# Two issuing queues and a re-scored order for the first loads of an attention kernel with two MLPs

## The chip, the cores and the metric

The kernel runs on one core of a Trainium2 chip. The metric is device time in microseconds (us), the median of several runs; lower is better. PE is the matrix engine (TensorE), DVE is VectorE, ACT is ScalarE, POOL is GpSimd, SP is SyncE, whose only work here is to start DMA transfers. Each engine runs its own list of instructions strictly in order; semaphores make one engine wait for another or for a transfer.

## What is computed

A strided sparse attention (4 batches, 8 heads, 576 tokens, 64 wide) feeds two MLPs one after the other. Half of the heads see the last 32 tokens, the other half every 32nd token.

```python
scores = scale * np.matmul(q, k.transpose(0, 1, 3, 2))
mask_local = (rel >= 0) & (rel < stride)
mask_strided = (rel >= 0) & (pos[None, :] % stride == pos[:, None] % stride)
...
attn = np.exp(scores - max); attn = attn / (sum + 1e-09)
x = (attn @ v), heads side by side          # 2304 tokens x 512
h = x @ w_in;  g = s * relu(h)**2 + b;  x = g @ w_out          # 512 -> 2048 -> 512
h = x @ w_in2; g = where(h >= 1, h, where(h <= -1, 0, (h + 1)**2 / 4)); out = g @ w_out2
```

## The kernel before

All matrix products of the MLPs are done three times on pairs of a high and a low part (hi*hi, hi*lo, lo*hi), so that float32 accuracy comes out of a faster matmul format. Lines 843 to 845 are these three in the first MLP, 1088 to 1090 in the later stages. Weights arrive as 64-bit numbers in tiles named `raw` (512 KB each, three buffers, loaded at L439) and are decoded into a hi and a lo tile: ACT (L443, into `dt`), DVE (L445, L447), a copy to the hi tile (L424, on ACT or DVE), a subtraction to the lo tile (L459, on DVE or POOL). `w0...` tiles are w_in pieces, `w1...` tiles are w_out pieces.

The 2304 tokens are cut into six units of 384. Unit 0 can enter the first MLP only when five attention tiles are complete: three strided tiles of batch 0 (inputs `in_strd`) and two local ones (`in_loc`). I number them 0 to 4; tile 5 is the next local one, whose scores also use spare PSUM banks. An attention tile is a chain:

- scores on PE: a mask matmul (L721, L733) and many small ones (L726 strided, L741 local);
- softmax: row maximum (DVE L749), subtraction (DVE L752), exponential (ACT L755), row sum (DVE L756), reciprocal (DVE L757), product (L758, DVE or POOL);
- transpose on PE (L767), copy to `pt` (L424);
- times the values on PE (L783 strided, L793 local);
- split into `xh` (ACT, L424) and `xl` (DVE, L826).

The third strided tile takes its keys and queries from small tiles `k` and `q`, filled by three DMAs and by POOL copies out of tiles 0 and 1. The inputs of the first tiles borrow buffers meant for later data, so load targets carry names such as `xh`, `xl`, `w0hx`, `w1hx`: `xh` and `xl` receive keys and queries, `w0hx`, `w0lx`, `w1hx`, `w1lx` receive values. The function `load` (L568) issues all of them on SP.

Nothing of the order is written by hand. Every step is recorded by `Issue.op` with its possible engines and an estimated length; `order` walks the steps back from the end to give each a due time; `draw` then simulates the engines 96 times with random shifts of the due times, always taking the step that can start first (earlier due time on a tie), and the draw whose PE ends first is emitted by `emit`. The simulation also holds a model of PE's clock (`Pulse`), and where PE would wait in the first 45 us it puts up to `MOST` matmuls on a constant tile (`busy`, L715, `warm_t`), which keep PE active and compute nothing. Ten more of these open the program (L1320). In `emit`, SP's loads planned for the first 32 us (`CALM`) also wait for an earlier load, so that not too much is in flight. Apart from that, each transfer uses one of eight completion semaphores in turn (DMAHW0 to DMAHW7), and one that reuses a semaphore may first wait until the transfer that used it last has landed.

## Time and profile before

| | us |
|---|---|
| median of three runs | 827.94 (826.4 to 828.8) |
| the profiled execution, whole | 829.0 |
| its span in the trace | 827.2 |
| PE busy | 813.6 (98%) |
| DVE busy | 627.0 (76%) |
| ACT busy | 516.4 (62%) |
| POOL busy | 113.5 (14%) |

The profiled execution's own time is 1.8 us above its span; that part lies outside the trace. Busy PE time contains the fillers of L715 and L1320 and every matmul that ran at the lower clock, so it is not all useful work. In the chain of work that ended last, PE has 94%, DMA 3%, SP's issuing 1% and ACT 1%. Times below count from the start of the span.

### The profile page before, as it was taken

Reading aid. Unit: us, or ns where it says so; the run is one execution under the profiler, and the core shown is the slowest. Engines: PE = TensorE matmul, PEld = TensorE weight load, DVE = VectorE, ACT = ScalarE, POOL = GpSimd, SP = SyncE. Lnnn points to the kernel's source line nnn. Section 1 sums busy time; section 2 is a strip of 40 time slices with the busy share of each in tenths; the row PEclk is TensorE's granted clock in tenths of the full one; section 3 lists DMA queues with packets and bytes.
Section 4 is the critical chain, followed back from the end, with each engine's and each line's share of the span. In section 5 each row is a group of like instructions: output and inputs, shape, how many; then the busy total and the mean of one; then the engine's idle time right before and its main releaser. Section 6 shows DMA issues by size and latency. Waiting matters only on the chain.

```text
span 827.2 us, 17722 instructions
## 1 busy us (share of the span) xinstructions
PE 813.6 (98%) x6295; PEld 788.1 (95%) x6301; DVE 627.0 (76%) x1314; ACT 516.4 (62%) x1052; POOL 113.5 (14%) x233
## 2 busy tenths in 40 slices
PE   7998999999999999999999999999999999999998
PEld 3688999999999999999999999999999999999998
DVE  4888429888867468689889987997477987466966
ACT  2576445565656676558676677855486855667553
POOL 4041104343321013030221000000000000000000
PEclk8999999999999999999999999999999999999999
DMA  6895265899777467899989999888988789888882
GB/s 222 269 300 189 86 204 178 277 298 302 270 267 255 149 238 268 299 305 351 340 307 337 294 399 353 253 251 274 305 253 254 253 251 298 282 253 253 253 267 95
DMA packets 105524, 218.25 MB, mean 264 GB/s; under 512 B 14196, under 2 KB 27868, under 8 KB 105436
## 3 DMA queue, kind: packets, MB, share of 16 engines
q1 hardware_dynamic: 95196, 180.41, 67.4%
q0 software_dynamic: 10240, 36.71, 11.8%
q8 instruction: 51, 0.84, 0.4%
q14 instruction: 37, 0.30, 0.1%
HBM read 170.93 MB, written 46.14 MB: 262 GB/s over the span
## 4 chain that ended last, share of the span: by engine, by line
PE 94%; DMA 3%; SPq 1%; ACT 1%; POOL 0%; issue 0%; DVE 0%; ACTq 0%
PE acc L1088 8%; PE acc L1090 8%; PE acc L1089 8%; PE h L843 8%; PE h L845 8%; PE h L844 8%; PE side L1088 6%; PE side L1090 6%; PE side L1089 6%; PE acc L843 4%; PE acc L844 4%; PE acc L845 4%; PE h L1088 3%; PE h L1090 3%; PE h L1089 3%; PE side L793 1%
## 5 line engine op out<-in xcount | busy, mean ns | idle before, releaser
L843 PE MATMUL h<-xh,w0hx 128*128 128x384 f32 x192 | 65.9, 343 | 1.4 <-ACT w0hx L424 1.4
L845 PE MATMUL h<-xh,w0lx 128*128 128x384 f32 x192 | 65.0, 339 | 0.8 <-POOL w0lx L459 0.8
L843 PE MATMUL h<-xh,w0h 128*128 128x384 f32 x192 | 65.6, 342 | 0.0
L489 POOL DMA_DIRECT2D dw<-pp x60 | 43.5, 725 | 155.7 <-DVE pp L487 129.4
L844 PE MATMUL h<-xl,w0hx 128*128 128x384 f32 x192 | 64.7, 337 | 0.0
L845 PE MATMUL h<-xh,w0l 128*128 128x384 f32 x192 | 64.4, 335 | 0.0
L844 PE MATMUL h<-xl,w0h 128*128 128x384 f32 x192 | 64.3, 335 | 0.0
L871 ACT ACTIVATE t<-h 128x384 f32<-128x384 f32 x50 | 24.5, 490 | 45.7 <-PE h L845 45.5
L883 DVE TENSOR_TENSOR gl<-t,gh 128x384 fp32r<-128x384 f32 x36 | 20.0, 555 | 26.9 <-ACT gh L424 26.9
L843 PEld LDWEIGHTS h<-xh,w0hx 128*128 128x128 f32 x192 | 36.1, 188 | 2.2 <-ACT w0hx L424 1.7
L845 PEld LDWEIGHTS h<-xh,w0lx 128*128 128x128 f32 x192 | 36.2, 189 | 1.2 <-POOL w0lx L459 1.1
L843 PEld LDWEIGHTS h<-xh,w0h 128*128 128x128 f32 x192 | 36.1, 188 | 0.5
L844 PEld LDWEIGHTS h<-xl,w0hx 128*128 128x128 f32 x192 | 36.2, 189 | 0.0
L844 PEld LDWEIGHTS h<-xl,w0h 128*128 128x128 f32 x192 | 36.1, 188 | 0.0
L845 PEld LDWEIGHTS h<-xh,w0l 128*128 128x128 f32 x192 | 36.0, 188 | 0.0
L424 ACT ACTIVATE gh<-w1h 128x384 fp32r<-128x384 f32 x48 | 24.9, 523 | 16.2 <-PE acc L1090 6.8
L1135 DVE TENSOR_TENSOR gl<-w1h,gh 128x384 fp32r<-128x384 f32 x48 | 26.5, 555 | 11.1 <-ACT gh L424 10.9
L843 PE MATMUL acc<-gh,w1h 128*128 128x384 f32 (+1 forms) x96 | 33.5, 349 | 0.0
L843 PE MATMUL acc<-gh,w1hx 128*128 128x384 f32 (+1 forms) x96 | 32.9, 343 | 0.0
L845 PE MATMUL acc<-gh,w1l 128*128 128x384 f32 (+1 forms) x96 | 32.5, 339 | 0.3 <-POOL w1l L459 0.3
L844 PE MATMUL acc<-gl,w1hx 128*128 128x384 f32 (+1 forms) x96 | 32.6, 339 | 0.0
L845 PE MATMUL acc<-gh,w1lx 128*128 128x384 f32 (+1 forms) x96 | 32.5, 338 | 0.0
(608 smaller groups left out, 2812.2 us busy)
## 6 DMA issues: line engine op xcount, KB each, us to landing
dw<-pp POOLq DMA_DIRECT2D x60, 512.0 KB, 5.2
w0h<-dw SPq DMA_DIRECT2D x84, 256.0 KB
w0l<-dw SPq DMA_DIRECT2D x84, 256.0 KB
w0hx<-dw SPq DMA_DIRECT2D x84, 256.0 KB
w0lx<-dw SPq DMA_DIRECT2D x84, 256.0 KB
raw<-in_w_ins SPq DMA_DIRECT2D x32, 512.0 KB
raw<-in_w_outs SPq DMA_DIRECT2D x32, 512.0 KB
kb<-dw SPq DMA_DIRECT2D x56, 256.0 KB
```

The lines of the kernel that those rows point to most:

```text
L424: e.activation(out=out, in_=in_, func=AF.Copy)
L489: op(lambda e: e.dma_start(out=dw[o][i][qs].rearrange("q p w n -> p q (w n)"), in_=y.tile[:, 0:nq].bitcast(F32).rearrange("p q w n -> p q ...
L793: e.matmul(out=pv[blk].tile[half(par), hp, c:c + 32], lhsT=v4(pos)[half(blk), s, 2 * hp + par, :], rhs=pt.tile[half(blk), 2 * par + pos, r ...
L843: e.matmul(out=acc, lhsT=wh, rhs=ah, start=first, stop=False)
L844: e.matmul(out=acc, lhsT=wh, rhs=al, start=False, stop=False)
L845: e.matmul(out=acc, lhsT=wl, rhs=ah, start=False, stop=last)
L871: op(lambda e: e.activation(out=c(t), in_=c(p), func=AF.Relu), [act(n)], [p], [t])
L883: op(lambda e: e.tensor_tensor(out=c(gl), in0=c(t), in1=c(gh).bitcast(F32), op=SUB), [pool(n)] + [dve2(n)], [t, gh], [gl])
L1088: e.matmul(out=dst, lhsT=wh, rhs=ah, start=opens and first, stop=False, skip_group_check=not opens)
L1089: e.matmul(out=dst, lhsT=wh, rhs=al, start=False, stop=False, skip_group_check=not opens)
L1090: e.matmul(out=dst, lhsT=wl, rhs=ah, start=False, stop=last, skip_group_check=not opens)
L1135: op(lambda e, g=g, hi=hi, lo=lo: e.tensor_tensor(out=lo.tile[:, 0:n], in0=g.tile, in1=hi.tile[:, 0:n].bitcast(F32), op=SUB), [dve2(n)], [ ...
```

## The change

Four things change, all in the planner and in `load`:

1. Loads of at most 128 KB that belong to tiles 0 to 2 may be issued by ACT as well as SP; the planner picks the engine that is free first.
2. The loads of the first unit are no longer kept in the fixed sequence `EARLY`: each target tile has a line of its own (`own`), and due times decide. Later loads stay in one line.
3. Of the 96 draws the best 24 are kept, each is replayed with five positions of the clock model's window, and the lowest sum wins. In the replay SP may run further ahead (`AHEAD_SP`).
4. Constants of the model: `MOST` from 8 to 12, ACT's start from 1.4 to 1.2, `FETCH` from 4.5 to 4.0, a limit on open transfers (`LANES`), and a longer issue time for small transfers.

```diff
-DRAWS, JITTER = 96, 1.0
+DRAWS, JITTER, KEPT, PHASES, AHEAD_SP = 96, 1.0, 24, (0.0, 0.7, 1.4, 2.0, 2.7), 4.0
-FILL, MOST = 45.0, 8
+FILL, MOST = 45.0, 12
...
-BEGIN = {"sp": 0.7, "act": 1.4, "dve": 0.5, "pool": 6.4, "pe": 5.2}
+BEGIN = {"sp": 0.7, "act": 1.2, "dve": 0.5, "pool": 6.4, "pe": 5.2}
...
-BLOCK, FETCH, FETCH_AT, FETCH_LONG = 256, 4.5, 1.5, 1.3
-CALM, FLIGHT = 32.0, 2.5
+BLOCK, FETCH, FETCH_AT, FETCH_LONG = 256, 4.0, 1.5, 1.3
+CALM, FLIGHT, LANES = 32.0, 2.5, 8
...
-        return min((self.draw(seed) for seed in range(DRAWS)), key=lambda x: x[0])[1]
+        drawn = sorted((x for x in map(self.draw, range(DRAWS)) if x[1]), key=lambda x: x[0])[:KEPT]
+        return min((sum(self.replay(took, phase) for phase in PHASES), n, took) for n, (_, took) in enumerate(drawn))[2]
...
+    def earliest(self, o, e, more, t, deep):
+        free = self.free
+        at = max(free[e], o.ready, t)
+        if "port" in more:
+            at = max(at, free["port"])
+        elif more and e != "pool":
+            at = max(at, self.lanes[-LANES])
+        if e == "sp":
+            at = max(at, free["dma"] - deep)
...
+    def replay(self, took, phase):
+        self.begin(phase)
+        for o in sorted(self.ops, key=lambda o: (took[o][0], o.n)):
+            _, e, n = took[o]
+            _, d, lag, *more = next(x for x in o.engs if x[0] == e)
+            self.put(o, e, self.earliest(o, e, more, self.room(o), AHEAD_SP), d, lag, more, n)
+        return self.free["pe"]
...
     def load(i, y, parts, size, piece):
         first = bool(w_loads) and not held
-        o = op(lambda e: [e.dma_start(out=f(), in_=x) for f, x in parts], [dma(size, piece, len(parts))], part=[y],
-               line=a_line, after=[w_loads[k] for k in HOLD] if first else ())
+        issue = (0.45 if size > 128 * 1024 else 0.62) * len(parts)
+        queues = ("sp", "act") if i < 3 and size <= 128 * 1024 else ("sp",)
+        o = op(lambda e: [e.dma_start(out=f(), in_=x) for f, x in parts], [dma(size, piece, 0.0, issue, q) for q in queues], part=[y],
+               line=a_line if brought else own.setdefault(y, []), after=[w_loads[k] for k in HOLD] if first else ())
```

The order moves at three places that matter here. In the changed program line numbers are 23 higher from `load` on.

**The first loads.** On SP, before, the first loads of the program stand like this; `in_strd` and `in_loc` are the attention inputs, and the sizes are partitions x float32 words:

```order
L568 DMA xh5_1_189<-in_strd 128x764 x2
L568 DMA xl5_2_192<-in_strd 128x2x764
L568 DMA w0hx_3_194<-in_strd 64x2x256 x2
L568 DMA k3_4_219<-in_strd 64x2x72 x2
L568 DMA q3_5_222<-in_strd 128x2x72
L568 DMA w0lx_6_227<-in_strd 64x2x256 x2
L568 DMA w1hx_7_257<-in_strd 18x256 x2
L568 DMA w1hx_7_257<-in_strd 64x256
L568 DMA w1hx_7_257<-in_strd 54x1x256
L568 DMA xh4_8_271<-in_loc 128x896
L568 DMA xl4_9_280<-in_loc 128x896
```

In the changed program SP has this at the same place:

```order
L591 DMA xh5_1_189<-in_strd 128x764 x2
L591 DMA xl5_2_195<-in_strd 128x2x764
L591 DMA xh4_8_234<-in_loc 128x896
L591 DMA xl4_9_274<-in_loc 128x896
L591 DMA xh3_12_285<-in_loc 128x896
L591 DMA xl3_13_315<-in_loc 128x896
L591 DMA xl2_57_334<-in_loc 128x896
L591 DMA xh2_56_399<-in_loc 128x896
```

And ACT, ahead of its first exponential (L778, L755 before), now has these, with the semaphores that they wait for:

```order
L591 DMA k_4_192<-in_strd 64x2x72 x2
L591 DMA q_5_197<-in_strd 128x2x72
L591 DMA w0hx_199<-in_strd 64x2x256 x2
L591 DMA w0lx_202<-in_strd 64x2x256 [waits DMAHW1_49]
L591 DMA w0lx_202<-in_strd 64x2x256 [waits DMAHW3_49]
L591 DMA w1hx_227<-in_strd 18x256 [waits DMAHW4_49]
L591 DMA w1hx_227<-in_strd 18x256 [waits DMAHW5_49]
L591 DMA w1hx_227<-in_strd 64x256 [waits DMAHW7_49]
L591 DMA w1hx_227<-in_strd 54x1x256 [waits DMAHW0_49]
L778 ACTIVATE sm_207<-sm_207 128x4x128 [waits DVE_49]
```

All eleven small loads of tiles 0 to 2 moved to ACT, and the six big loads of tiles 3 to 5 follow the strided ones directly on SP. The semaphore DMAHW3 is that of the load of `xl5`, the last DMAHW0 that of `xh4`.

**PE around the second step of the first MLP.** `h_80` is that step's result, `h_64` and `sx_62` belong to tile 5, `warm_t` is the filler. Before, between the second step and the values of tile 5:

```order
L845 MATMUL h_80_781<-xh0_177,w0l_77_510 128x384
L715 LDWEIGHTS warm_t_73
L715 MATMUL h_64_816<-warm_t_73 128x512
...
L767 MATMUL h_64_816<-id_t_69,sx_62_702 128x128 x4
...
L715 MATMUL side_66_836<-warm_t_73 128x512
...
L793 MATMUL side_66_836<-pt_65_817,qx_58_748 64x32 x2
```

Now the second step is followed by the scores of a later strided tile and then by the third step:

```order
L868 MATMUL h_80_786<-xh0_177,w0l_77_565 128x384
L744 LDWEIGHTS idb_t_72
L744 MATMUL side_172_816<-bias_t_71,idb_t_72 128x256
...
L749 MATMUL side_172_816<-xh5_168_762 54x54
...
L866 MATMUL h_88_846<-xh0_177,w0h_84_680 128x384
L867 MATMUL h_88_846<-xl0_178,w0h_84_680 128x384
```

The fillers there are gone, and the transpose of tile 5 now stands ahead of the first step.

**ACT at the decoding of the seventh w_in piece.** `raw_138` is its load, `raw_146` is a w_out piece, `w0hx_136` the hi tile made from the first. Before:

```order
L443 ACTIVATE dt_139_1154<-raw_138_1052 128x512
L443 ACTIVATE dt_147_1172<-raw_146_1107 128x512
L755 ACTIVATE sx_193_1122<-sx_193_1122 128x4x128
L871 ACTIVATE t_129_1148<-h_128_1147 128x384
L875 ACTIVATE t_129_1148<-t_129_1148 128x384
L424 ACTIVATE w0hx_136_1053<-dt_139_1154 128x512
```

Now:

```order
L898 ACTIVATE t_129_1144<-t_129_1144 128x384
L445 ACTIVATE gh_130_1145<-t_129_1144 128x384
L445 ACTIVATE w0hx_136_1065<-dt_139_1172 128x512
L464 ACTIVATE dt_147_1225<-raw_146_1116 128x512
L778 ACTIVATE sx_193_1182<-sx_193_1182 128x4x128
```

The copy into `w0hx_136` moved from behind the instruction that waits for `raw_146` to ahead of it.

## Rows read from the trace of the kernel before

**Rows 1.** Windows: length, busy PE PEld DVE ACT POOL, clock, DMA share, GB/s.

```profile
0.00:36.57 36.57, 29.00 (x584) 17.45 (x589) 23.29 (x65) 14.43 (x36) 10.13 (x45) 0.91 0.75 246
36.57:75.00 38.43, 35.90 (x390) 31.63 (x386) 31.28 (x69) 27.08 (x60) 12.72 (x22) 0.96 0.87 253
75.00:823.50 748.50, 748.45 (x5330) 739.02 (x5328) 571.91 (x1180) 474.66 (x957) 90.64 (x166) 1.00 0.80 266
```

**Rows 2.** Waits of PE: total us, times, longest.

```profile
PE acc L741 <- DMA xh<-in_loc: 2.8, 1, 2.8
PE h L843 <- ACT w0hx L424: 1.4, 1, 1.4
PE acc L741 <- DMA xl<-in_loc: 1.1, 1, 1.1
PE h L845 <- POOL w0lx L459: 0.8, 1, 0.8
```

**Rows 3.** SP's issues in order of time: start, us, line, transfer, count.

```profile
1.65 0.43 SPq L568 DMA_DIRECT2D xl<-in_strd  x1
4.00 1.95 SPq L568 DMA_DIRECT2D w0hx<-in_strd  x2
9.24 2.32 SPq L568 DMA_DIRECT2D w1hx<-in_strd  x4
12.10 0.41 SPq L568 DMA_DIRECT2D xl<-in_loc  x1
```

**Rows 4.** Timeline of the prologue: start, us, what, idle before and releaser.

```profile
7.96 0.21 POOL L426 COPY k<-xl 64x36 f32<-64x36 f32 x1 [1.24 <-DMA xl<-in_strd]
8.10 0.63 ACT L755 ACTIVATE sm<-sm 128x512 f32<-128x512 f32 x1 [5.87 <-DVE sm L752]
9.34 0.68 DVE L756 TENSOR_REDUCE mx<-sm 128x8 f32<-128x520 f32 x1
34.94 0.88 DVE L826 TENSOR_TENSOR xl<-side,xh 128x128 fp32r<-128x128 f32 x4 [0.28 <-ACT xh L424]
36.57 0.44 PE L843 MATMUL h<-xh,w0h 128*128 128x384 f32 x1
```

**Rows 5.** DVE alone from its first row sum to its last split: window, waits.

```profile
9.34:35.82 26.48, 19.74 (x55) 0.87 0.79 256
DVE xl L826 <- ACT xh L424: 2.9, 4, 1.0
DVE mx L749 <- PE acc L741: 2.9, 1, 2.9
```

**Rows 6.** Windows, DMA share and rate before, around and after the prologue.

```profile
6.80:13.60 6.80, 4.87 (x79) 2.88 (x77) 5.97 (x17) 1.86 (x3) 2.68 (x14) 1.00 0.52 128
13.60:37.40 23.80, 19.35 (x464) 13.02 (x469) 16.85 (x46) 11.08 (x31) 2.84 (x6) 0.86 0.84 280
37.40:60.00 22.60, 22.25 (x247) 19.69 (x250) 18.27 (x39) 16.81 (x36) 8.08 (x17) 1.00 1.03 287
70.00:73.60 3.60, 3.60 (x42) 3.06 (x41) 3.40 (x10) 2.47 (x8) 0.03 (x1) 0.53 0.75 192
```

**Rows 7.** Timeline of PE behind the second step of the first MLP.

```profile
40.84 0.82 PE L715 MATMUL h<-warm_t 128*128 128x512 bf16 x2
41.50 0.60 PE L767 MATMUL h<-id_t,sx 128*128 128x128 f32 x4
41.94 1.03 PE L715 MATMUL side<-warm_t 128*128 128x512 bf16 x4
```

**Rows 8.** Timeline around PE's wait for the seventh w_in piece.

```profile
61.95 0.67 ACT L443 ACTIVATE dt<-raw 128x512 f32<-128x512 f32 x1 [1.03 <-DMA raw<-in_w_ins]
64.97 0.67 ACT L443 ACTIVATE dt<-raw 128x512 f32<-128x512 f32 x1 [2.34 <-DMA raw<-in_w_outs]
67.00 0.61 ACT L424 ACTIVATE w0hx<-dt 128x512 fp32r<-128x512 f32 x1
67.66 0.45 PE L843 MATMUL h<-xh,w0hx 128*128 128x384 f32 x1 [1.43 <-ACT w0hx L424]
```

More of the change, by code (lines that the diff above doesn't have):

```diff
@@ L238, in draw @@
             for x in o.engs:
[L239 removed]
+                self.free[x[0]] = BEGIN.get(x[0], 0.0)
             for b in o.bufs:
[L241 to L254 removed]
+                b.left, b.end, b.near = len(b.users), 0.0, 0.0
@@ new lines, in earliest, with put @@
+    def earliest(self, o, e, more, t, deep):
[7 more added lines that the diff above has]
+            at = max(at, free["dma"] - deep)
+            if at < CALM:
+                at = max([at, *(end for line, end in self.flight if free["dma"] - line >= FLIGHT)])
+        return at
+    def put(self, o, e, at, d, lag, more, n=None):
+        free = self.free
+        if e == "pe":
+            n, at, d = self.pe.run(o, free[e], at, d, n)
+            if self.pe.fetched is not None and at < FILL:
+                free["slow"], self.pe.fetched = max(free["slow"], self.pe.fetched + FETCH_AT) + FETCH_LONG, None
+        free[e] = at + d
+        end = at + d + lag
+        if "port" in more:
+            free["port"] = at + d
+        elif more:
+            for line in ("dma", "slow"):
+                free[line] = max(free[line], at + more[2]) + more[1]
+            end = max(at + d, free["dma"], free["slow"]) + lag
+            if e != "pool":
+                self.lanes = [*self.lanes[1:], end]
+            if e == "sp" and at < CALM:
+                self.flight = [*self.flight[-11:], (free["dma"], end)]
+        for b in o.allocs:
+            b.ring.taken.append(b)
+        for b in o.bufs:
+            b.left -= 1
+            b.end = max(b.end, end + LATENCY)
+            b.near = max(b.near, at + d if e == "pe" else end + LATENCY)
+        for q in o.succ:
+            q.wait -= 1
+            q.ready = max(q.ready, at if o in q.behind else at + d if q.engs[0][0] == e == "pe" else end + LATENCY)
+        return at, n or 0
@@ new lines, in room, with draw @@
+    def room(self, o):
+        t, more = 0.0, {}
+        for b in o.allocs:
+            n = len(b.ring.taken) + more.get(b.ring, 0) - b.ring.bufs
+            more[b.ring] = more.get(b.ring, 0) + 1
+            if n >= 0:
+                if n >= len(b.ring.taken) or b.ring.taken[n].left:
+                    return None
+                t = max(t, b.ring.taken[n].near if o.engs[0][0] == "pe" else b.ring.taken[n].end)
+        return t
+    def draw(self, seed):
+        rng = np.random.default_rng(seed)
+        self.begin(PHASE)
+        for o in self.ops:
+            o.due = o.base + JITTER * rng.standard_normal()
+        pool, took = [o for o in self.ops if not o.wait], {}
@@ L293, in draw @@
-            for b in o.allocs:
-                b.ring.taken.append(b)
-            for b in o.bufs:
-                b.left -= 1
-                b.end = max(b.end, end + LATENCY)
-                b.near = max(b.near, at + d if e == "pe" else end + LATENCY)
-            for q in o.succ:
-                q.wait -= 1
-                q.ready = max(q.ready, at if o in q.behind else at + d if q.engs[0][0] == e == "pe" else end + LATENCY)
-                if not q.wait:
-                    pool.append(q)
```

89 lines of the change are left out of this document (26 added, 63 removed).

## The prediction

> **What bounds the kernel now.** I read the windows by stage first. From 75 to 823.5 us PE is busy 748.45 of 748.50 us at full clock [rows 1]; nothing that other engines do there can shorten the kernel, and the change removes no matmul of the MLPs. All that can be won lies in the first 75 us: the first unit's first matmul of the MLP stands at 36.57 us [rows 4], and up to there PE mostly waits or runs fillers, though it reads as 29.00 us busy [rows 1]. So the question is when that matmul starts, and what PE loses between it and 75 us.
>
> The waits of PE name the losses: 2.8 and 1.1 us for the first local loads (`in_loc`), then 1.4 and 0.8 us for a decoded weight [rows 2]. The local loads are late because SP issues them late: the small strided loads stand ahead of them and take about 0.6 us each to issue (1.95 us for two with a wait in it, 2.32 us for four), so that `xl4` is issued at 12.10 us [rows 3]. Meanwhile the DMA engines are half idle: share 0.52 and 128 GB/s from 6.8 to 13.6 us, against 0.84 and 280 GB/s later [rows 6]. The change goes at exactly this. What matters is which wait comes in its place.
>
> **Term 1, the start of the MLP.** On the other side of the move is ACT. It now has eleven issues ahead of its first exponential, which ran at 8.10 us [rows 4]. Before it can run, three things must be over.
>
> First, the seventh issue waits for `xl5`. That load landed at 7.96 us [rows 4]. Ahead of it on the DMA engines are now up to 0.55 MB of small loads, which stood behind it before: at the 280 GB/s of a busy stretch [rows 6] up to 1.9 us, but ACT can only issue them at one per 0.6 us from about 2.3 us on, so part comes too late to be in the way. I take 8.7, with bounds 7.96 and 9.9.
>
> Second, that issue and the four after it: one at 0.6 and 2.32 us, the price of the same four on SP [rows 3]. No row of before shows an issue on ACT, so the price is that of the nearest rows; it could be as low as nothing if ACT hands off faster (then the exponential follows at 8.7), or the 0.98 of the dearer SP row, half of 1.95 [rows 3], which gives 4.9 instead of 2.9. Third, the last issue also waits for the first local load (semaphore DMAHW0), 0.46 MB behind `xl5`: at 280 GB/s 1.6 us later, at 10.3, inside the 2.9 us and therefore free.
>
> So the first exponential starts at 8.7 + 2.9 = 11.6 and ends at 12.3, and the row sum of tile 0 on DVE, in before at 9.34 [rows 4], starts at 12.3: three microseconds later. DVE's order behind it is fixed, and that is the chain to follow. From that row sum to its last split of unit 0, DVE had 19.74 us of work in 26.48 us [rows 5]. By the two orders the new list has one softmax more (tile 5, with the pieces 0.76, 0.76, 0.68, 0.2 and 0.7: 3.1 us), one product of 0.69 less and the two early pieces of a third weight (1.1) less: 21.0 us. The gaps of 6.7 us in before were 2.9 for the local loads, 2.9 for four `xh` copies of ACT, and small ones [rows 5]. The first goes: the local loads now leave SP within the first 6 us, and are needed only when PE reaches their scores near 16. Of the other 3.8 I keep 3.0, since the splits still follow ACT's copies. 12.3 + 21.0 + 3.0 = 36.3, and PE can start the MLP at 36.4. Before, the last split ended at 35.82 and PE was held until 36.57 by the scores of tile 5, which now come earlier. **Term 1: -0.2 us.** Its bounds: 8.7 + 0.7 + 21.0 + 2 = 32.4 if issuing on ACT is free, or 9.9 + 4.9 + 0.7 + 21.0 + 3.8 = 40.3 if everything is dear: -4.2 to +3.7.
>
> **Term 2, fillers between the steps.** Behind the second step PE ran fillers from 40.84 to 41.50 and again 1.03 us from 41.94, around the transpose of tile 5 [rows 7], because tile 5's softmax was late: 0.66 + 1.0 us. In the new order the transpose stands ahead of the first step, which also takes its 0.44 us out of this stretch, and the scores of a strided tile fill the place; their load is the nineteenth on SP and has some 25 us to land. **Term 2: -2.1 us**, bounds 0 and -2.1.
>
> **Term 3, the wait for the seventh w_in piece.** PE lost 1.43 and 0.75 us at 67 to 69 us, and then ran 3.6 us at a granted clock of 0.53 [rows 6, 8], the lower level of 1.2 GHz, which cost 3.6 x 0.47 = 1.7 us. The 1.43 is not a late load: the piece itself was in ACT at 61.95. ACT then stood for 2.34 us at the instruction that waits for the next w_out piece, and the copy that PE needed came behind it, at 67.00 [rows 8]. In the new order that copy stands ahead of the w_out instruction. What is late next is the piece itself. Up to it, by the shapes in the two orders, 15.4 MB (in units of 1024 KB) have to be loaded, the same as before. The loads are ahead by (280 - 128) x 6.8 = 1.03 MB [rows 6], or 3.6 us at 287 GB/s, the rate of 37.4 to 60 us, where the engines were full (share 1.03) [rows 6]. PE wants it some 2.3 us earlier (terms 1 and 2). So supply keeps about 1.3 us in hand; I count 3.0 of the 3.9 as saved. **Term 3: -3.0**, bounds 0 and -3.9.
>
> The Trainium skill, on the page "DMA: Bandwidth & Descriptors", section "Issuing engines are not separate DMA queues", says that issuing from several engines only saves sequencer time, which is usually small beside the transfer. Here the trace disagrees in size: issuing at 0.6 us each beside a DMA share of 0.52 is what holds the line from 4 to 12 us [rows 3, 6]. By the page alone term 1 would lose its gain and keep its cost.
>
> The re-scored draws, the window phases and the larger `MOST` change nothing that runs except the order; fillers on PE fall from 53 to 44 and lie in waits. Behind 75 us the same matmuls follow each other in a slightly different order, and other engines have slack there; I cost this at zero. If that cover fails, a wait like those of rows 2 (0.8 to 1.4) is the price.
>
> **The sum.** -0.2 - 2.1 - 3.0 = -5.3. Against the profiled execution (829.0, of which 827.2 is the span) that is 823.7. That execution is 1.1 above the median of the three runs, and a median taken from 827.94 would be 822.6. I stay near the first, at 823.8: the clock dip of term 3 is something that the typical run need not pay in full, so less than 5.3 may come back.
>
> **Rivals.**
> - *Prologue freed as well.* Issues on ACT are cheap and `xl5` is not delayed: term 1 goes to about -3.0. For it: nothing shows the price on ACT. Against it: SP's rows are steady. 829.0 - 3.0 - 2.1 - 3.0 = 820.9. Chance 0.14.
> - *Weights set the pace.* PE asks for weights 2.3 us earlier while the DMA share there is already 1.03 [rows 6]; the 1.03 MB in hand is lost to SP's own waits for raw buffers, and term 3 comes back as a wait elsewhere with its clock dip. 829.0 - 2.3 = 826.7, no measurable change. Chance 0.20.
> - *One descriptor generator.* ACT's and SP's issues exclude each other, each small load waiting for a big one's 0.43 us [rows 3]: three times on the chain, 1.3 us. 823.8 + 1.3 = 825.1. Chance 0.06. The Trainium skill, "Perfetto Trace Analysis", section on the HWDGE DMA instruction, describes such a lock, with the time spent in it shown as part of the issue; no row of before can show it, since one engine alone issues.
> - *The clock falls in the prologue (slower).* The late first exponential leaves PE only short fillers between 9 and 14 us; it falls to the lower level and stays there until the MLP starts. The stretch from 13.6 to 37.4 had 19.35 us busy at a mean clock of 0.86 [rows 6]; all of it at 0.5 would be 33.3 us, 13.9 more, of which the 4.45 us of idle time there absorb a part. 829.0 - 5.3 + 9.5 = 833.2. It decides if that stretch is granted less than about 0.65: then the added time exceeds the 6.6 us that lie between 823.8 and 830.4. For it: the stretch already dips. Chance 0.10.
>
> **Chances.** The forecast has 0.50. A measurement of this kernel can tell about 0.3% from no change, 2.5 us: below 825.4 is faster, above 830.4 slower. Faster: nearly all of the forecast's share (0.45), the first rival and most of the third: 0.64. Same: the weights rival and what is left: 0.27. Slower: the last rival, most of it: 0.09. The range runs from the freed prologue, 820.8, to a partly lost prologue or a full loss of terms 2 and 3 with term 1 slightly positive, 828.3.
>
> **What would show it.** In the new profile: ACT's first exponential near 11.6; the wait of PE for `in_loc` gone; the first matmul of L866 (L843 before) near 36.4; no filler behind it; PE's waits for decoded weights under 1 us in total and no clock below 0.9 between 60 and 75 us. I am wrong if ACT starts before 10 (too pessimistic), or if DVE's last split comes after 38, or if a new wait for weights of over 2 us stands between 45 and 75 us.

## The result: slower by about one per cent

| | before | after |
|---|---|---|
| median of the runs, us | 827.33 (826.4 to 828.8, 4 runs) | 835.62 (834.81 to 836.68, 4 runs) |
| profiled execution, us (its span) | 829.0 (827.2) | 836.17 (834.4) |

The ratio is 1.0099, 95% interval 1.0078 to 1.0121. On a second chip, later, it was 1.0059 (1.0016 to 1.0101). The forecast was 823.8 with a range to 828.3: the sign is wrong.

Where the time went is read from one simple table. Every trace holds the same 4248 matmuls of the MLPs, so the start of the n-th of them (counted from 0 in order of time) says how far the kernel has come. After minus before, in us:

| matmul | 0 | 24 | 120 | 144 | 156 | 168 | 240 | 720 | 2820 | 4080 |
|---|---|---|---|---|---|---|---|---|---|---|
| before, at | 36.57 | 43.96 | 67.66 | 76.42 | 78.61 | 80.70 | 96.18 | 205.45 | 574.90 | 794.19 |
| after, later by | 1.96 | 1.34 | 1.55 | 0.30 | 5.30 | 6.96 | 4.49 | 4.83 | 6.46 | 6.98 |

The start is two microseconds late, this is gone by matmul 144, and then 6.7 us are lost between 76 and 88 us. (It is gone against this profile of before, which has a stall there; two later profiles of before, at the end of the experiments, lack it, and at matmul 144 after is 2.1 and 2.6 behind them.) Part of that is no loss: without the fillers, the new order has done 928 attention matmuls by matmul 168 where before had done 794, and by matmul 240 both have done 932. So 4.5 at matmul 240 is the net loss up to there. Of the 2.7 us that follow, 0.3 come by matmul 720 and 1.4 between 720 and 2400, 0.9 of them in one wait for a weight load at 488 us; 1.0 lies in the pace of the last part (below).

The windows of after, by stage (answering to [rows 1]; the columns are the same), and lines of the view of waits, of PE (answering to [rows 2]; the third is from 100 us on):

```profile
0.00:38.50 38.50, 29.54 (x584) 18.19 (x590) 22.47 (x65) 13.76 (x35) 11.06 (x47) 0.91 0.79 234
38.50:75.00 36.50, 32.98 (x433) 29.48 (x434) 31.95 (x70) 26.77 (x58) 10.60 (x18) 1.00 0.96 286
75.00:100.00 25.00, 22.55 (x201) 21.29 (x200) 16.26 (x34) 12.10 (x27) 8.75 (x15) 0.93 0.58 171
```

```profile
PE h L790 <- POOL sx L777: 4.4, 1, 4.4
PE side L744 <- DVE xl L849: 3.6, 3, 2.4
...
PE side L1111 <- DMA w0l<-dw: 0.9, 1, 0.9
```

The old waits for the local loads and for the decoded `w0hx` are gone. Two new ones stand in their place: 4.4 us in the prologue and 2.4 us at 82 us.

**The prologue.** The timeline of ACT, after (answering to [rows 4]; ACTq is ACT's issuing of DMAs, a row may hold several with the waits between them), VectorE's last split (DVE), and PE's first MLP matmul. The last three of the four `w1hx` issues stand once more by themselves:

```profile
3.33 1.26 ACTq L591 DMA_DIRECT2D w0hx<-in_strd  x2
5.00 5.08 ACTq L591 DMA_DIRECT2D w0lx<-in_strd  x2
10.12 4.41 ACTq L591 DMA_DIRECT2D w1hx<-in_strd  x4
14.57 0.63 ACT L778 ACTIVATE sm<-sm 128x512 f32<-128x512 f32 x1 [12.34 <-DMA w0lx<-in_strd]
...
38.34 0.89 DVE L849 TENSOR_TENSOR xl<-side,xh 128x128 fp32r<-128x128 f32 x4 [1.28 <-ACT xh L445]
38.53 0.44 PE L866 MATMUL h<-xh,w0h 128*128 128x384 f32 x1 [0.70 <-ACT xh L445]
```

```profile
10.91 0.28 ACTq L591 DMA_DIRECT2D w1hx<-in_strd  x1
13.14 0.50 ACTq L591 DMA_DIRECT2D w1hx<-in_strd  x1
13.68 0.84 ACTq L591 DMA_DIRECT2D w1hx<-in_strd  x1
```

An issue that does not wait takes about 0.6 us (two for `w0hx` in 1.26). The second `w0lx` issue stood until `xl5` had landed, at 9.45 by the trace. The third `w1hx` issue, which waits for semaphore DMAHW7, stood for 2 us until the second small load of `w0hx` had landed, at 13.12, 9 us after its own issue. The last one followed at once: the first local load (DMAHW0) had landed at 12.74. So the first exponential ran at 14.57 instead of 8.10. On the changed kernel's second profile the third issue stood until 14.52 in the same way.

**The stretch at 80 us.** SP's issues in time, ACT's conversions of raw weights (L464; L443 before), the wait of PE, and the window behind it:

```profile
67.95 0.53 SPq L591 DMA_DIRECT2D xh<-in_strd  x1
68.59 0.40 SPq L460 DMA_DIRECT2D raw<-in_w_outs  x1
69.31 1.88 SPq L591 DMA_DIRECT2D qx<-in_loc  x2
72.22 0.33 SPq L460 DMA_DIRECT2D raw<-in_w_outs  x1
72.71 0.39 SPq L591 DMA_DIRECT2D xl<-in_strd  x1
73.17 1.30 SPq L591 DMA_DIRECT2D k<-in_strd  x2
76.00 0.33 SPq L460 DMA_DIRECT2D raw<-in_w_outs  x1
```

```profile
78.08 0.67 ACT L464 ACTIVATE dt<-raw 128x512 f32<-128x512 f32 x1 [2.23 <-DMA raw<-in_w_outs]
80.18 0.66 ACT L464 ACTIVATE dt<-raw 128x512 f32<-128x512 f32 x1 [1.43 <-DMA raw<-in_w_outs]
80.74 0.61 ACT L778 ACTIVATE sm<-sm 128x512 f32<-128x512 f32 x1
81.26 0.66 ACT L445 ACTIVATE xh<-side 128x60 fp32r<-128x60 f32 x4
...
82.58 0.57 PE L744 MATMUL side<-bias_t,idb_t 128*128 128x256 bf16 x2 [2.40 <-DVE xl L849]
```

```profile
84.00:88.00 4.00, 4.00 (x14) 4.00 (x15) 3.35 (x8) 1.23 (x3) 3.86 (x12) 0.57 0.65 192
```

The raw piece issued at 68.59 was converted at 78.08, the one issued at 72.22 at 80.18. ACT works in order: behind those waits stood the `xh` copies from which PE's next scores are released. PE then stood still for 2.40 us, and behind that the granted clock was 0.57 for four microseconds, near the lower level of 1.2 GHz.

Why do the pieces come so late? The view of the DMA engines from 60 to 82 us, after (two lines) and before (one):

```profile
DMA packets 3153, 6.60 MB, mean 300 GB/s; under 512 B 748, under 2 KB 1365, under 8 KB 3150
...
raw<-in_w_outs SPq DMA_DIRECT2D x4, 512.0 KB, 9.4
```

```profile
DMA packets 1861, 4.60 MB, mean 209 GB/s; under 512 B 266, under 2 KB 522, under 8 KB 1858
```

The new order moves two megabytes more in these 22 us, with the engines full (busy share 1.03 against 0.65). The 9.4 us from issue to landing are those of one raw piece, that of 68.59; by the conversions that waited for them, those of 72.22 and 76.00 took some 8 and 9. The extra bytes are attention data. Most are the next batch's strided tile: `xh`, `xl`, `k` and `q`, which before issues from 99.8 us on and whose first scores run at 129.1 us in after. Two causes are thus in question, and the runs take them apart: **issues on ACT that wait for a landing**, and **the early fetch** of that tile.

### The profile page after: what moved, and what is told of

The parts are those of the page before. It is cut to its first block, busy times and chain, and to the rows that moved or that the text cites. A ratio compares the mean times of both kernels' runs of the same rounds, so it can differ in the third digit from the quotient of the medians.

```text
span 834.4 us, 17726 instructions
## 1 busy us (share of the span) xinstructions
PE 814.6 (98%) x6286; PEld 789.6 (95%) x6292; DVE 629.5 (75%) x1307; ACT 519.5 (62%) x1055; POOL 122.6 (15%) x237
## 4 chain that ended last, share of the span: by engine, by line
PE 89%; DMA 7%; DVE 2%; issue 1%; ACT 1%; SPq 0%; POOL 0%; ACTq 0%; POOLq 0%; DVEq 0%
PE acc L1113 8%; PE acc L1112 8%; PE acc L1111 8%; PE h L866 8%; PE h L868 7%; PE h L867 7%; PE side L1111 6%; PE side L1112 6%; PE side L1113 6%; PE acc L866 4%; PE acc L867 4%; PE acc L868 4%; PE h L1112 3%; PE h L1111 3%; PE h L1113 3%; DMA raw<-in_w_ins 2%
## 5 line engine op out<-in xcount | busy, mean ns | idle before, releaser
L464 ACT ACTIVATE dt<-raw 128x512 f32<-128x512 f32 x42 | 27.6, 664 | 10.6 <-DMA raw<-in_w_outs 6.1
```

Of the source, the lines that this page charges most:

```text
L464: first = op(lambda e: e.activation(out=x(), in_=words(1).bitcast(F32), func=AF.Prelu, scale=2.0 ** -112, alpha=-2.0 ** 32), [act(DM)], [r ...
```

## The experiments

Ratios are to runs of the kernel before on the same chip in the same hour, with the 95% interval; most executions of one kernel lie within 3 us of their median, so single profiles show mechanisms and medians show sizes. "Order" means the instructions of every engine in their frozen sequence; the plan's operations are moved in it by number.

**The queue alone: all small loads back on SP** (`a1_loads_on_sync`)

```diff
+ operations 3 to 10 (k, q, w0hx, w0lx, w1hx): engine "act" -> "sp", same planned times
```

> The order of the changed kernel on every engine, but its eight small first loads (k, q, w0hx, w0lx, w1hx) stand in SyncE's queue at their planned starts instead of ScalarE's. Theory (ScalarE's queue held the first exponential, 14.57 us against 8.10 in the kernel before): the first exponential comes back to 8 to 10 us and the first MLP matmul from 38.53 us to 36.5 to 37.5 us; the wait of TensorE at 82.6 us, which the theory puts down to something else, stays, and the time falls by 1 to 2 us to 833.5 to 834.5. Rival one (small packets and large ones disturb each other in the DMA engines whichever queue issues them): the first exponential stays behind 12 us and the time within 1 us of 835.6. Rival two (one cause for everything, the loads on ScalarE): the wait at 82.6 us goes too and the time comes to 827 to 829.

831.59 us, ratio 1.0034 (1.0018 to 1.0050). First exponential at 8.39, MLP at 37.15. The stall at the weights stays:

```profile
78.94 0.57 PE L744 MATMUL side<-bias_t,idb_t 128*128 128x256 bf16 x2 [2.15 <-DVE xl L849]
```

From matmul 144 to 168 this kernel loses 6.2 us against before, as after does (6.7); to matmul 240, where the attention done is the same, it is 4.0 and 4.2. So the queue makes the late start and the stall has another cause. The gain, from 1.0099 or 1.0059, is 2 to 5 us, larger than the start alone. And 0.34% stay that the queue does not explain.

**The five blocked issues behind the exponentials** (`a2_issues_later`)

```diff
+ 8 (w0lx, second half): 4.92 -> 8.9;  9, 10 (w1hx): 5.54, 7.54 -> 11.40, 11.42 (ScalarE)
```

> The order of the changed kernel, but of ScalarE's eleven small DMA issues the last five (the second half of w0lx, the four of w1hx) stand behind the first exponential (one) and behind the second (four). Theory (ScalarE works in order, and these five issues, of which two waited for a landing, kept it from the exponential): the first exponential starts at 9.5 to 11 us instead of 14.57, the first MLP matmul at 36.8 to 37.8 us instead of 38.53; the wait at 82.6 us stays, and the time falls by 0.5 to 1.5 us to 834 to 835. Rival (the transfers are slow, not the issues: TensorE and VectorE wait for xl and xh4 anyway): the exponential comes early but the first MLP matmul stays within 0.4 us of 38.5, and so does the time of 835.6.

A miss: 837.38 us, 1.0102 (1.0072 to 1.0132). The exponential came early, at 7.76, and then the moved issues blocked what now stood behind them. ACT's rows and PE's wait for it:

```profile
15.07 7.07 ACTq L591 DMA_DIRECT2D w1hx<-in_strd  x4
22.19 0.60 ACT L445 ACTIVATE pt<-h 128x512 f32<-128x512 f32 x1 [8.36 <-DMA w1hx<-in_strd]
...
22.84 1.11 PE L806 MATMUL side<-pt,w0hx 54*64 54x54 f32 x32 [8.06 <-ACT pt L445]
```

The MLP started at 42.43. The mechanism is the forecast one, only stronger: an issue that has to wait is harmful wherever it stands on ACT. By matmul 144 this kernel was only 0.98 behind, and at matmul 240 it was 0.9 ahead of after: a start 3.9 us later than after's is worked off while the weights are awaited.

**The `xh` copies ahead of the second conversion** (`a3_copies_between`, and with the edit above `a4_both`)

```diff
+ 399, 401 (xh copies, ScalarE): 72.37, 72.82 -> 71.55, 71.56;  318 (conversion): 71.02 -> 71.59
+ 400, 402 (xl, VectorE): 73.26, 73.58 -> 71.60, 71.61
```

> The order of the changed kernel, but near 79 us ScalarE's four copies of attention values into xh stand ahead of the second of the two conversions of raw w_outs pieces (and the exponential behind it), and VectorE's four subtractions into xl that follow them move along. Nothing else moves. Theory (ScalarE waited 1.43 us for the transfer of the second piece while TensorE's next scores waited 2.40 us for those copies, and TensorE then ran at a granted clock of 0.55 to 0.59 from 84 to 88 us): the wait of 2.40 us falls under 1 us, the low clock goes or shortens, the delay at the 168th MLP matmul falls from 7.0 us to 2 to 5 us, and the time falls by 2 to 4.5 us to 831 to 833.5. Rival (the weights are late by then, and TensorE only meets them a little later): the matmuls wait for w1hx instead, and the time stays within 1 us of 835.6.

831.31 us, 1.0032 (1.0007 to 1.0058), within the expected time, but the trace speaks for the rival. The wait for `xl` is gone and PE meets the same late pieces three steps on:

```profile
81.18 0.44 PE L866 MATMUL acc<-gh,w1hx 128*128 128x384 f32 x1 [1.29 <-ACT w1hx L445]
82.59 0.69 PE L868 MATMUL acc<-gh,w1lx 128*128 128x384 f32 x1 [0.80 <-DVE w1lx L480]
```

Its profiled execution, 835.10, lies at the upper end of its ten runs (828.22 to 835.35), so how much the edit is worth stays open; the lateness of the weights does not.

> Both edits of the two runs ahead: the five late issues behind the exponentials, and the four copies into xh ahead of the second conversion. Theory (two separate causes that add): the sum of the two gains, 829.5 to 832.5. Rival (both meet the same later limit, the weights): no better than the better of the two alone, 831 to 835.

836.17 us, 1.0097 (1.0069 to 1.0125): the harm of the later issues outweighs it.

**Eleven issues on ACT in the order of before** (`b1_before_loads_on_act`)

```diff
+ kernel before: operations 3 to 10: engine "sp" -> "act", at the changed kernel's times
```

> The order of the kernel before on every engine, but its eight small first loads (eleven issues) stand in ScalarE's queue at the places they have in the changed kernel. Theory (issues on ScalarE that wait for a landing keep its first exponential, and what stands behind it): the first exponential falls back from 8.10 to 12.5 to 15 us and the first MLP matmul from 36.57 to 38 to 40 us; the order behind it is that of before, so of this only what the old waits at 67 to 69 us absorb is won back, and the time rises by 1 to 4 us to 829.5 to 832.5. Rival (the queue is harmless in an order that is made for it or not, and the loss of the changed kernel is its new order): the time stays within 1 us of the kernel before.

829.95 us, 1.0024 (0.9999 to 1.0049); the trace shows the same picture, with the first exponential at 15.79 and the MLP at 38.69:

```profile
11.19 4.50 ACTq L568 DMA_DIRECT2D w1hx<-in_strd  x4
15.79 0.63 ACT L755 ACTIVATE sm<-sm 128x512 f32<-128x512 f32 x1 [13.55 <-DMA w1hx<-in_strd]
```

So the estimate for the queue in the old order is about 2 us too, but its interval (0 to 4) just reaches none.

**Only the first six issues** (`a5_six_on_act`), of which five wait for nothing and the sixth for an early load (it ran at 5.27 us)

```diff
+ 8, 9, 10 (second half of w0lx, w1hx): "act" -> "sp", behind SyncE's fourth load
```

> The order of the changed kernel, but of ScalarE's eleven small issues only the first six (k, q, w0hx, the first half of w0lx), which waited for nothing, stay there; the five that waited or stood behind a wait (second half of w0lx, w1hx) go to SyncE behind its fourth load. Theory (an issue that waits for a landing is what costs, not the queue itself): the first exponential at 7.5 to 9 us, no issue on ScalarE behind it, the first MLP matmul at 35 to 37.5 us instead of 38.53, the time at 830 to 833, no worse than with all loads on SyncE (831.6). Rival (two queues disturb each other's transfers): first MLP matmul later than 38 us, time 834 to 837.

832.06 us, 1.0036 (1.0009 to 1.0062). Exponential at 7.81, MLP at 34.70: 3.8 us earlier than after and 1.9 earlier than the first profile of before. The early start is lost again at the weights (from 4.61 ahead at matmul 144 to 2.43 behind at 168), and the time equals that with all loads on SP.

**The attention loads behind the last raw pieces** (`c1_attention_loads_late`, `c2_late_and_six`)

```diff
+ 533 to 536 (qv, qx), 764, 793 (xh, xl), 765 (k): from 59.6 to 68.6 -> 69.90 to 69.94 (SyncE)
```

> The order of the changed kernel, with its loads on ScalarE, but seven loads of attention data (qv, qx, xh, xl and k, about 2.1 MB, wanted from about 91 us on) stand in SyncE's queue behind the last three pieces of raw w_outs of the first unit instead of ahead of and between them. Theory (from 60 to 82 us the DMA engines moved 6.6 MB against 4.6 in the kernel before, at a busy share of 1.03; the raw pieces took 9.4 us to land behind it, and ScalarE and TensorE waited for them): the raw pieces land within 4 to 6 us of their issue, ScalarE's waits for raw of 2.23 and 1.43 us and TensorE's of 2.40 us go, the clock stays at full, the first MLP matmul stays at 38.5, and the time falls by 3 to 5 us to 830.5 to 832.5. Rival (the order of ScalarE's and VectorE's instructions alone makes the wait): the raw pieces land earlier but the time stays within 1.5 us of 835.6.

834.81 us, 1.0084 (1.0059 to 1.0110): a miss that showed the other half. The raw pieces were converted at 72.14 and 73.64 without a wait for them. But the tile's small copies kept their places, and now they were what waited. ACT's row and PE's:

```profile
83.69 0.23 ACT L445 ACTIVATE k<-xl 64x36 f32<-64x36 f32 x1 [7.68 <-DMA xl<-in_strd]
...
85.26 0.44 PE L866 MATMUL acc<-gh,w1hx 128*128 128x384 f32 x1 [2.84 <-ACT w1hx L445]
```

A copy of 0.23 us, wanted over 40 us later, held ACT for 7.68 us, and behind it stood the copy of `w1hx` that PE needed. (The profiled execution, 831.30, was the fastest of its nine.)

> Both of the edits of the two runs ahead: six issues on ScalarE and five on SyncE, and the seven attention loads behind the last raw pieces. Theory (two causes, a late start and a late supply, which add): the first MLP matmul at 35 to 37.5 us, no wait above 1 us from 60 to 90 us, the time at 825 to 829, at or a little under the kernel before. Rival (the earlier start meets the same supply, so the gains overlap): 829 to 832.

833.86 us, 1.0051 (1.0022 to 1.0079), with the same wait (PE 3.58 us for `w1hx` at 86.10).

**The tile's loads and its twelve copies late** (`c3_prefetch_and_copies_late`, `c4_prefetch_late_and_six`)

```diff
+ as above for 533 to 536;  764, 793, 765, 766 (loads) -> 96.0 (SyncE)
+ 769 to 774, 796 to 801 (copies k, q) -> 97.0 (GpSimd, ScalarE)
```

> The order of the changed kernel, with its loads on ScalarE, and the edit of the run with late attention loads carried through: the strided tile of the next batch (loads xh, xl, k, q and the twelve small copies of it on GpSimd and ScalarE, whose values TensorE wants only near 126 us by the plan) is moved behind 96 us, where the kernel before has it too (its loads are issued there from 99.8 us); qv and qx stand behind the last raw piece. Theory (what the changed order lost in the stretch from 60 to 100 us is the early fetch of that tile: its bytes kept the raw pieces waiting, and with the raw pieces ahead ScalarE waited 7.68 us in order at a 0.23 us copy of it): no wait of ScalarE or TensorE above 1 us from 60 to 90 us, full clock there, the first MLP matmul still at 38.3 to 38.8, the delay against the kernel before at the 240th MLP matmul under 0.5 us instead of 4.5, the time at 829 to 832. Rival (the first unit is bound by the decoding of its weights on ScalarE, VectorE and GpSimd, whatever else is moved): waits for w1hx stay at 1 us and more, the time at 833 to 836.

829.12 us, 1.0013 (0.9995 to 1.0032): with the eleven issues still on ACT and the MLP still starting at 38.60, 4 to 7 us of the loss are gone. No wait of PE above 0.3 us is left from 60 to 90 us and the clock stays at full. The windows of this run:

```profile
78.00:82.00 4.00, 3.90 (x99) 3.21 (x95) 3.97 (x11) 2.92 (x9) 0.00 (x0) 1.00 0.66 194
82.00:86.00 4.00, 4.00 (x25) 4.00 (x24) 3.78 (x10) 1.44 (x3) 1.83 (x2) 1.00 0.74 210
```

At matmul 240 it is 0.60 behind the profiled execution of before, where after was 4.49 behind; what was expected was under 0.5. The edit also moves `qv` and `qx`; what the tile alone is worth was not tried.

> The edit of the run with the next batch's strided tile moved late, and of the eleven small issues on ScalarE only the first six there, the other five on SyncE. Theory (late start and early fetch are the whole loss, and the new list of ScalarE's queue is worth what was predicted of it once nothing waits in it): first MLP matmul at 34 to 35.5 us, delay at the 240th MLP matmul -2 to -4 us, the time at 823 to 827, faster than the kernel before. Rival (what is won at the start is lost at the weights again): 828 to 831.

828.42 us, 1.0001 (0.9987 to 1.0015). The MLP starts at 34.20, matmul 240 stands 4.55 us ahead of the profiled execution of before. The first was expected, the second went a little beyond the 2 to 4 expected; the time was not expected: it equals before's. The last part of this section and the account below come back to that.

**The two halves of the rest** (`p1_replanned_sync_only`, `p3_first_draw`)

```diff
- queues = ("sp", "act") if i < 3 and size <= 128 * 1024 else ("sp",)
+ queues = ("sp",)                      # first run: planned anew, SyncE only
- return min((sum(self.replay(took, phase) for phase in PHASES), n, took) ...)[2]
+ return drawn[0][1]                    # second run: best draw of the single phase
```

> The changed kernel with one part of the change left out: the small loads may go through SyncE's queue only, and the plan is made anew by the changed rules (due dates of the first loads, five clock phases). Theory (the rules of the order, not the queue, move the next batch's tile forward): the first exponential near 8 to 9.5 us; whether a wait comes back at 66 to 86 us depends on where the new order puts that tile; 828 to 833. Rival (the queue is the whole loss): the time within 1 us of the kernel before or under it, 825 to 829.

831.33 us, 1.0038 (1.0023 to 1.0053).

> The changed kernel with another part left out: the order is the draw that the plan's own single clock phase scores best, as in the kernel before, and not the best over five phases; loads on ScalarE and the new due dates stay. Theory (ScalarE's waiting issues cost about 2 us at the start in any such order, and which order is chosen adds from 0 to 4 us by chance): first exponential at 12 to 15 us, time 829 to 836. Rival (the choice over five phases is what went wrong): 826 to 829.

833.35 us, 1.0059 (1.0038 to 1.0079); exponential at 14.98. Both plans issue the next batch's tile early as well (`xh` at 62.47 and 67.18) and move 6.07 and 6.08 MB from 60 to 82 us. So neither the ACT queue nor the choice over five phases is needed for bringing it forward; other changed rules of the plan may do it. Which does was not tried, nor both parts left out together. Nor does fetching it early always hurt: the plan for SP alone, which puts `xh` and `xl` ahead of 64.7 us, goes from matmul 144 to 240 in 19.6 us, where before takes 19.8 and after 23.9. Its MLP starts at 38.50; what else makes that plan slower was not found.

**The copies alone, and the early fetch in the order of before** (`c5_copies_late_alone`, `b2_before_early_fetch`)

> The order of the changed kernel, with its loads on ScalarE and all loads at their places, but the twelve small copies of the next batch's strided tile (ten on GpSimd, two on ScalarE) are moved behind 97 us. Theory (in the changed order the bytes do the harm, since the raw pieces took 9.4 us to land; the copies do it only where the raw pieces go first): ScalarE still waits 2 us and more for raw w_outs, TensorE 2 us near 82 us, the time within 1.5 us of the changed kernel, 833 to 837. Rival (the copies in the way of ScalarE and GpSimd are the cause): the wait at 82 us falls under 1 us and the time to 829 to 831.

835.73 us, 1.0098 (1.0062 to 1.0133), ACT waiting 2.79 us for raw and PE 2.67 us at 81.89: with all loads where the changed kernel has them, moving the twelve copies away wins nothing.

```diff
+ kernel before: 764, 793, 765, 766 (loads): 94.65 to 98.16 -> 63.14 to 68.80, around the raw pieces
+ the twelve copies: 99.4 to 103.5 -> 73.6 to 76.25
```

> The order of the kernel before, all small loads on SyncE, but the next batch's strided tile (loads xh, xl, k, q of about 1.6 MB, and its twelve copies) stands where the changed kernel has it: its loads ahead of and between the last three raw w_outs pieces, its copies behind them. Theory (the early fetch is the larger cause of the loss): first MLP matmul still at 36.6, a new wait of ScalarE for raw pieces or for the tile of 2 us and more and of TensorE of 1 us and more between 72 and 88 us, the delay at the 240th MLP matmul 2.5 to 6 us, the time at 831 to 835. Rival (the early fetch hurts only after a late start, or only in the changed order): within 1.5 us of the kernel before.

829.66 us, 1.0026 (1.0007 to 1.0046): about 2 us, less than expected, and the rival's 1.5 is within the interval. The mechanism is there, and from matmul 144 to 240 this profile (833.77, the slowest of its ten) takes 24.0 us, as long as after (23.9). ACT, then PE:

```profile
80.50 0.66 ACT L443 ACTIVATE dt<-raw 128x512 f32<-128x512 f32 x1 [4.57 <-DMA raw<-in_w_outs]
...
82.22 0.44 PE L843 MATMUL acc<-gh,w1hx 128*128 128x384 f32 x1 [1.36 <-ACT w1hx L424]
```

**Six issues on ACT in the order of before, and the changed kernel again** (`b3_before_six_on_act`, `after2_same_chip`)

```diff
+ kernel before: 5, 6, 3, 4, 7 (k, q, w0hx, first half of w0lx): "sp" -> "act"
```

> The order of the kernel before, but the first six of the small issues (k, q, w0hx, first half of w0lx) go through ScalarE at the places they have in the changed kernel; the other five stay on SyncE. Theory (issues on ScalarE that wait for nothing are free, and SyncE issues the local loads some 4 us earlier): first exponential at 7.5 to 9.5 us, the local loads' waits of TensorE (2.8 and 1.1 us) go, the first MLP matmul at 34.5 to 36.3 us; what is won there is lost again in part at the weights, the time at 826 to 828.5 where the kernel before stands at 828.5, too little to tell. Rival (the order behind is fixed to the old landing times and gains nothing): first MLP matmul within 0.5 us of 36.57.

827.84 us, 1.0004 (0.9981 to 1.0026): nothing that can be told. The MLP started at 37.07, not earlier: `xl5` came late, beside the earlier small transfers, and PE waited 3.01 us for it.

> The changed kernel itself, for its time on the chip and in the hour of these runs. Theory: 1% over the kernel before as measured first, 836 to 838 where the kernel before stands at 828.5, with the two waits of ScalarE for raw w_outs near 80 us as in the first profile. Rival (the first measurement was of a chip that suits it ill): within 0.5% of the kernel before, 828 to 833.

833.01 us (830.60 to 836.95), 1.0059 (1.0016 to 1.0101): the loss is there on another chip, with the same two waits of ACT for raw (2.27 and 1.80 us) in its profile. The interval covers the first result but reaches down to almost nothing.

**Was the profiled execution of before a typical one?** (`before2_profile`, `before2_profile_again`)

> The kernel before, unchanged, profiled once more. Theory (the profiled execution from which the third term was read is worse in that place than most, so the 3.0 us counted there are not all in the median): the wait for w0hx near 67 us is under 1 us or the granted clock behind it stays above 0.9, the 144th MLP matmul at 72.5 to 75 us instead of 76.42, and the even part from matmul 2820 to 4080 takes 219.8 us as in the other runs here, instead of 219.3. Rival (the first profile was typical): a wait of 1.2 us and more, the clock at 0.5 to 0.6 behind it, matmul 144 at 76 to 77 us.

> The same once more, since the wait may come in some executions and not in others. Theory: in one of the two at least the clock does not fall behind the wait, and matmul 144 stands at 72.5 to 75 us. Rival: both as in the first profile, matmul 144 at 76 to 77 us.

828.31 and 828.55 us. Matmul 144 stood at 74.14 and 74.66, not 76.42, matmul 240 at 93.91 and 94.43, not 96.18. Of the first of them, the waits at the place of [rows 8], and then the window of the dip in [rows 6]:

```profile
66.85 0.44 PE L843 MATMUL h<-xh,w0hx 128*128 128x384 f32 x1 [0.65 <-ACT w0hx L424]
68.21 0.44 PE L845 MATMUL h<-xh,w0lx 128*128 128x384 f32 x1 [0.74 <-POOL w0lx L459]
```

```profile
70.00:73.60 3.60, 3.60 (x47) 3.25 (x42) 3.60 (x11) 3.18 (x9) 0.00 (x0) 1.00 0.75 248
```

The clock did not fall. In the other, the wait for `w0hx` was under 0.3. The stall that the third term meant to win back was thus one execution's, some 2 us worse at matmul 240 than these. That execution made up for most of it: from matmul 720 to 2400 these two lose 1.8 and 1.6 us against it, among others in short waits for operands at 444 to 452 us, which it does not have. And the even part (below) took 219.29 in both, not the 219.8 expected, so that part of the theory fell.

## Why the prediction was wrong, step by step

**Term 1 failed by a wait that was not in it.** Forecast -0.2 us, measured +1.96 between the two first profiles. Single profiles spread, but the two groups stand apart: six with the first loads of after start the MLP between 38.34 and 39.86, four with those of before between 35.74 and 37.92. The price of an issue, 0.6 us, was right, and `xl5` landed at 9.45, inside the bounds given. Behind it the prediction counted one more landing, the local load's, at 10.3 and free. But each `w1hx` issue waits for a landing, and the third one waited for the second half of `w0hx`, a small load that ACT itself had issued at 3.98 and that landed at 13.12. So the four issues took 4.41 us instead of 2.32. The local load came at 12.74; by an estimate from these times it alone would have held the last issue about 1 us less. The DMA engines, half idle in before [rows 6], had a busy share of 1.08 here, and the estimate had let the load through at the rate of a busy stretch as if nothing else were in it. From the row sum on, the working held: DVE went from 15.24 to the end of its last split at 39.23, 24.0 us, as counted, and PE began on the high parts 0.7 us before that end. The value lies inside the stated bounds (-4.2 to +3.7).

On the rule of the Trainium skill that was weighed there ("DMA: Bandwidth & Descriptors", section "Issuing engines are not separate DMA queues": several issuing engines save only sequencer time): by it term 1 would lose its gain and keep its cost, and with eleven issues on ACT the start did come later, though for the waits above. With six it came at 34.20 to 34.70 in the changed order (37.15 with all on SP) and at 37.07 in the old one, so no general gain of a second queue is shown either.

**Term 2 was mostly lost.** From matmul 0 to 24 after won back 0.6 us, not 2.1. The strided tile's load, given "some 25 us to land", was issued at 35.86 and wanted 8 us later, and PE waited 0.98 us for it at 44.75. Another 0.6 went over the first 23 matmuls, where PE waited for `xl`.

**Term 3 is the step that turned the sign.** The wait for the seventh w_in piece did go: from matmul 120 to 144 after gained 1.25 us. But the supply was reckoned up to that piece only (the loads ahead by 1.03 MB), and the three w_outs pieces behind it were not followed. In this stretch, ahead of and between those, two megabytes more are moved than in before, most of them the tile that before fetches 30 us later. At 300 GB/s, the rate of this stretch, 2 MB are an estimated 6.7 us; the delay grows by 6.7 from matmul 144 to 168 and by 4.2 to matmul 240, where the attention done is the same. That the first two agree is luck in part. That what lies behind 75 us was costed "at zero", with 0.8 to 1.4 if the cover fails, is the same fault: the order was compared on PE and ACT around the old waits, and what SP issues from 60 to 82 us does not enter the sum. The rival "weights set the pace" (0.20) named the mechanism, a wait elsewhere with its clock dip; it was priced as a gain forgone, 826.7, though nothing kept it from costing more than the gain.

**The base was off as well.** The forecast stood on one profiled execution whose stall is not in the two others (above). With both causes out and six issues on ACT, matmul 240 is 4.55 us ahead of that execution, near the -5.3 of the sum, yet only 2.3 to 2.8 ahead of the other two. That 748.45 of 748.50 us were busy behind 75 us was that execution's as well: the two others lost 1.6 to 1.8 us between matmul 720 and 2400.

**And one microsecond was in no step.** From 600 to 790 us PE is busy for 190.00 us at full clock in every trace. The 1260 matmuls from 2820 to 4080 took 219.29 us in all six traces of the old order, 219.82 in all thirteen of the new and of the first-draw plan, and 219.54 in the plan made anew for SP alone, on whichever chip. The difference is not spread evenly: between the first profiles it grows from matmul 2560 to 2920, from 3250 to 3600 and from 3910 on, by 0.37, 0.24 and 0.37 us, and stands still between those. That is 1.0 us in all, none of it ahead of matmul 2400. No row shows the reason; it stays open. It explains only a part of why the kernel with six issues and no early fetch, 2.3 to 2.8 us ahead of the two later profiles at matmul 240, has before's median: its profile is still 2.0 to 2.3 ahead at matmul 4080, but at 826.55 it was among the fastest of its twelve executions. The rest stays open.

**The other rivals.** The prologue was not freed. A lock between the two issuing engines hardly shows: SP's issue of `xl5` took 0.43 us as before, and of ACT's issues only the first, 0.81 us beside one of SP's, is longer than the next (0.61). The clock fell no further in the prologue than before: 0.91 up to 38.5 us, as in [rows 1], and 0.86 from 13.6 to 37.4, as in [rows 6]; the chance of slower, 0.09, was hung on the wrong mechanism. (Its threshold of 0.65 leaves out the 4.45 us of idle time, of which its own sum lets a part be absorbed; with all of it the threshold is about 0.55.)

**What is shown and what not.** Shown by taking each away: waiting issues on ACT cost 2 to 5 us in the new order, and the early fetch with its copies 3 to 7 (after against the run with the tile late, and the two runs with six issues against each other). Putting each into the old order costs about 2 us; for the issues the interval just reaches no cost. The two overlap, since a late start is partly worked off while the weights are awaited: with the tile late, the same issues cost 1 us by the medians (1.0013 against 1.0001), which is within the noise. The place of the early fetch's loss is the same in both orders. From matmul 144 to 240 the five traces of the old order without it take 19.8 us and the one with it 24.0; in the new order after takes 23.9, its second profile 24.2, and the two with the tile late 20.1 both. Not settled: why the new rules fetch that tile early, what slows the plan made for SP alone, what the order of ACT's `xh` copies is worth by itself, and the even part's pace. No version ran faster than before.

## What to carry to other kernels

An engine that computes in order may issue a DMA cheaply, but not one that can wait: of eleven issues, the first six, which waited for little, kept nothing up, and the five others held the softmax for 6 to 8 us, ahead of its first exponential or behind it. When an order changes, add up the bytes that each queue has ahead of every weight the matmuls still need, to the last one and not only to the one that was late; a prefetch that is harmless by its due date can hold both the queue and, through its small copies, an engine. And profile the kernel before more than once before pricing a stall of one execution.

## What was not expected of the hardware

- With small transfers issued earlier on a second engine the big one beside them came later: in the order of before PE got `xl5` at 10.56 and 10.63 us with loads on ACT (two traces), and between 7.95 and 9.37 with all on SP (four traces). From 6.8 to 10.2 and from 10.2 to 13.6 us after's engines had a busy share of 1.09 and 1.08 at only 283 and 239 GB/s.
- A small load of 128 KB (the second half of `w0hx`) took 9.1 us from its issue to its landing in that stretch, and held the engine whose later issue waited for it.
- A raw piece of 512 KB took up to 9.4 us from issue to landing while 6.6 MB went through in 22 us.
- The same 1260 matmuls, without a wait and at full clock, took 219.29, 219.54 or 219.82 us depending on the order of the program alone, and the difference came in stretches of some 350 matmuls.
